# A three-part kernel on one core: the first expert told from one row of its batch, first rows loaded in 1 KB runs, last rows stored in another order, and a new list of steps

## Chip, cores and metric

The kernel runs on one core of a Trainium2 chip. The metric is the device time of one execution in microseconds; shorter is better. Engines are named as in the profile: PE is TensorE (its matmuls; PEld its weight loads), DVE is VectorE, ACT is ScalarE, POOL is GpSimd, SP is SyncE. A name with q (SPq, ACTq) is the engine's instruction queue, which issues transfers.

## What is computed

The reference, cut to what matters (B=4 batches, H=8 heads, S=512 rows, 32 state rows, D=64):

```
a      = softmax(x @ state^T / 8) ; xread = a @ state           # per batch and head
a2     = softmax(state @ x^T / 8) ; sread = a2 @ x
rows   = concat(xread, sread)  -> [4 * 544, 512]
expert = argmax(rows @ w_gate) ; gate = its softmax weight       # 8 experts, 576 places each
mid    = gate * (relu(rows @ w1[expert]) @ w2[expert])           # 512 -> 1024 -> 512; 0 for rows without a place
out    = (silu(mid @ wg) * (mid @ wv)) @ wo                      # 512 -> 1536 -> 512
```

All of it is float32.

## The kernel before

The path `one_expert_a_batch` bets that the 512 x rows of a batch all pick one expert, and its 32 state rows too. It works out these eight experts from counts over all rows, and counts at the end (`verdict`, line 1949) how many of its conditions held. If one did not, the register `bad` is above 0 and a second, general program (`general_path`, line 26) does everything again after it.

The work is cut into small **steps** (`lx`, `xt`, `up` and so on, with a batch number and mostly a piece number). Three lists written out by hand (lines 2311, 2362, 2379) fix the order in which every engine meets them: each engine runs its own instructions in list order and waits on the others only for data or for a free buffer. So a step that waits holds up all that stands behind it on its engine. Weight loads are all issued by SP, in list order as well.

**Attention.** `lx(b)` (line 1549) loads 512 rows of x: row 4p+c goes to partition p, slot c; it is four transfers, one for each c, in runs of 64 values (256 bytes) because x lies head by head. For batch 0 they are split over the SP and the ACT queue, and behind them ACT issues the gate's weights `wgt` and half of the other batches' states. `xt`/`xc` turn x (PE transposes, copies), `sc` makes the scores, `sx`, `mx`, `tt`, `ex2`, `sub`, `ae`, `sn`, `an`, `at`, `ah`, `al` make both softmaxes and split the weights in two float32r parts, `rd` (line 1713) reads x again for the state rows, `lg`, `lc`, `lt` and `ga` to `gf` make the gate's logits, the winner and the places. `ge` (line 1865) writes the expert's number into `e_i`. There are two x buffers (`f_xs`), so the load of batch 2 waits until `rd:0` has read batch 0.

**First expert layer.** `lu(b,z)` (line 1980) reads the expert's number into a register on SP and loads its w1 in four transfers of 512 KB; `ld` loads w2 in four. `z` is 0 for the batch's x rows and 1 for its state rows. `pj` multiplies the states with w1 (the layer is applied to 256 state columns first, since x rows are mixtures of states), `pa`/`pd` split the product, `up`, `hh`, `hl`, `wh`, `wl`, `dn` are the two matmuls in pieces of 128 hidden columns. The state rows take the narrow steps `n1` to `n4l`. A float32 product is three float32r matmuls of high and low parts (`mm3`, line 1464; the matmul itself has line 1466).

**Second layer.** `w2l` loads the 36 pieces of wg, wv, wo; `da`, `db`, `dc`, `dd` rebuild and split each (lines 2217 to 2255); they can begin only when the attention's buffers are given back after `verdict`. `fu`, `fs`, `fm`, `fh`, `fl`, `fd` run batch 0's rows against a piece as soon as it is split. After the lists, `block` (line 2424) runs batch 1, batch 2 and the rest (the last 64 of batch 2's rows, 64 rows of batch 3 and the 128 state rows), and `finish` copies and stores. The state rows stand in the tile `yF` batch after batch, and `rest_rows` stores them so:

```python
o = out.rearrange("(b s) d -> b s d", b=B)[:, S:SEQ]
for b in range(0, B, 2):
    (nc.scalar if b else nc.sync).dma_start(o[b:b + 2], t[NS * b:NS * (b + 2)])
```

Of the kernel before, what the change touches and what calls it, by code (L numbers as in the profile page):

```python
# [1395 lines left out]
def one_expert_a_batch(  # L1396
# [127 lines left out]
    act = ctile([1, 2], "act", pool=const)  # L1524
    nc.scalar.activation(act[:, 0:1], ione[:, 0, 0:1], AF.Exp)
# [22 lines left out]
    @step  # L1548
    def lx(b):

        v[b]["xs"] = xs = xsp.tile([P, NC, DM], F32, tag="xs", name="xs")
        for c in range(NC):
            (nc.scalar if b == 0 and c % 2 else nc.sync).dma_start(
                xs[:, c].rearrange("p (h d) -> p h d", h=H),
                x[b].rearrange("h (p c) d -> c p h d", c=NC)[c],
            )
        if b == 0:
            nc.scalar.dma_start(wgt, w_gate.rearrange("(k p) e -> p k e", p=P))
            for i in range(1, B):
                for g in range(2):  # L1560
                    (nc.scalar if g else nc.sync).dma_start(st_[:, 2 * i + g], state[i, g::2])
# [38 lines left out]
    @step  # L1600
    def xt(b, ks):

        ks = [ks] if b else range(KD)
        for k in ks:
            v[b]["pxt"][k] = bank([P, NC, P], b == 0)
        for c in range(NC):
            for k in ks:
                nc.tensor.transpose(
                    v[b]["pxt"][k][:, c], v[b]["xs"][:, c, k * P:(k + 1) * P], ident
                )  # L1610
# [253 lines left out]
    @step  # L1864
    def ge(b, z):

        n, t = rows_n(z)
        po = v[b]["pq", z]
        nc.vector.tensor_copy(tot[:, b, z], po[0:1, 0])
        w = sm.tile([1, E], F32, tag="t", name="t")  # L1870
        nc.vector.tensor_tensor(w, tot[:, b, z], ione[:, z], op=ALU.mult)
        u = sm.tile([1, 1], F32, tag="u", name="u")
        nc.vector.tensor_reduce(u, w, axis=AX.X, op=ALU.add)
        nc.vector.tensor_copy(e_i[:, 2 * b + z:2 * b + z + 1], u)
        v[b]["places", z] = pl = small(z, "pl", [n, E])
        nc.vector.tensor_copy(pl, po[0:n, 1])
# [433 lines left out]
    with tc.manual_schedule():  # L2310
        run("""
            lx:0 lx:1 st:0 stc:0 xt:0:0 xc:0:0 xc:0:2 st:1 xc:0:1 xc:0:3 xt:1:2 stc:1 sc:0 sg:1
            sx:0:0 mx:0:1 sx:0:1 mx:0:0 ex2:0:1 tt:0:1 ex2:0:0 sgc:1 et:0:1 sub:0:1 xt:1:0
            ec:0:1 rs:0 ae:0:1 et:0:0 xc:1:0 sn:0:1 xc:1:2 tt:0:0 ec:0:0 xt:1:1 an:0:1 sub:0:0
            rd:0 xc:1:1 ae:0:0 at:0:1 lx:2 sr:0 sn:0:0 xt:1:3 ah:0:1 qt:0 sg:0 qc:0 al:0:1
            xc:1:3 an:0:0 sl:0 sgc:0 at:0:0 ga:0:1 sc:1 ah:0:0 gx:0:1 al:0:0 sx:1:0 mx:1:0 lg:0
            sx:1:1 mx:1:1 ex2:1:0 tt:1:1 tt:1:0 sub:1:1 lc:0 et:1:0 ex2:1:1 lt:0 sub:1:0 ae:1:1
            et:1:1 ec:1:0 xt:2:0 ec:1:1 ga:0:0 xt:2:1 gb:0:0 ae:1:0 rd:1 xc:2:0 xc:2:1 gb:0:1
            pq:0:0 gx:0:0 xt:2:3 ge:0:0 pq:0:1 xc:2:3 xt:2:2 sn:1:1 lu:0:0 xc:2:2 ge:0:1 an:1:1
            sn:1:0 at:1:1 ah:1:1 rs:1 an:1:0 ld:0:0:0 gf:0:1 sr:1 ld:0:0:1 ld:0:0:2 qt:1 al:1:1  # L2320
            gd:0:1 at:1:0 qc:1 gf:0:0 pj:0:0 ah:1:0 gd:0:0 al:1:0 pj:0:1 pa:0:0:0 pa:0:0:1
            pd:0:0:0 wh:0:0 pd:0:0:1 wh:0:1 wl:0:0 wl:0:1 lg:1 pa:0:1:1 pa:0:1:0 pd:0:1:1
            pd:0:1:0 sl:1 lc:1 lt:1 ga:1:1 up:0:0 ga:1:0 gx:1:1 gb:1:0 gx:1:0 up:0:1 hh:0:0
# [223 lines left out]
```

## Time and profile before

| | us |
|---|---|
| three runs: median (lowest to highest) | 564.66 (564.31 to 565.61) |
| the profiled execution | 566.21 |
| its span, first to last instruction | 564.6 |
| PE busy in the span | 528.6 (94%) |
| DVE busy | 263.3 (47%) |
| ACT busy | 193.2 (34%) |

The span is what the rows are measured in; 1.6 us of the profiled execution lie around it. All times in rows count from the start of the span. Busy shares are averages over stages with different limits; the stretches tell them apart. PEclk is the granted clock of PE as a share of 2.4 GHz; 0.50 is 1.2 GHz.

### The profile page before, as it was taken

What the parts mean: (1) busy time and instruction counts of PE and PEld (TensorE: products, weight loads), DVE (VectorE), ACT (ScalarE), POOL (GpSimd) and SP (SyncE); (2) the same over time, 40 slices, a digit from 0 to 9 for tenths busy, and PEclk for the clock granted to TensorE, in tenths of its full rate; (3) what the DMA queues carried; (4) which work ended last, traced back from release to release, by engine and by line L of the source; (5) the groups of instructions that cost most, each with busy time, mean ns of one, the idle gap of its engine ahead of it and who ended that gap; (6) DMA issues with size and microseconds to landing.
All of it is one profiled execution on the core that took longest, in us unless ns stands there. A gap on an engine that the chain in (4) does not pass through costs nothing.

```text
span 564.6 us, 8671 instructions
## 1 busy us (share of the span) xinstructions
PE 528.6 (94%) x3402; PEld 430.4 (76%) x3402; DVE 263.3 (47%) x601; ACT 193.2 (34%) x372; POOL 31.7 (6%) x52
## 2 busy tenths in 40 slices
PE   4877999999999997999999999999999999999990
PEld 2654777777787875778888888888888888899990
DVE  2586564657565895799997211111121112231120
ACT  1563444454454653565553211111121111121110
POOL 1110010221030021000000000000000000000000
PEclk9997999999999999999999999999999999999996
DMA  8146694688563978887755500000220000010001
GB/s 162 24 111 210 208 324 134 151 269 287 173 241 128 361 256 259 268 291 212 244 182 165 207 0 1 0 1 0 71 79 2 0 1 0 1 66 1 1 1 43
DMA packets 66968, 72.51 MB, mean 128 GB/s; under 512 B 20389, under 2 KB 51877, under 8 KB 66661
## 3 DMA queue, kind: packets, MB, share of 16 engines
q1 hardware_dynamic: 63634, 70.92, 39.8%
q10 hardware_dynamic: 3282, 0.93, 0.8%
q8 instruction: 29, 0.48, 0.4%
q14 instruction: 23, 0.18, 0.1%
HBM read 62.14 MB, written 9.70 MB: 127 GB/s over the span
## 4 chain that ended last, share of the span: by engine, by line
PE 80%; DVE 7%; DMA 5%; ACT 2%; issue 1%; SPq 1%; POOL 1%; ACTq 1%; POOLq 0%; DVEq 0%
PE m L1466 57%; PE py L1466 13%; DMA rawb<-in_moe_w_dram 2%; DVE hv L2227 1%; DMA yd<-y 1%; DMA f_wgt<-in_moe_w_gate_dram 1%; PE m L2151 1%; PE m L2115 1%; PE py L2453 1%; PE m L1624 1%; DMA rawa<-in_moe_w_dram 1%; DVE hv L2230 1%; DMA xs<-in_x_dram 1%; DVE w L2255 1%; DVE t L2071 1%
## 5 line engine op out<-in xcount | busy, mean ns | idle before, releaser
L2441 DVE TENSOR_TENSOR sg<-sg,m 128x512 f32<-128x512 f32 (+2 forms) x36 | 20.8, 577 | 161.3 <-PE m L1466 161.3
L1466 PE MATMUL m<-xbh,w 128*128 128x512 f32 (+1 forms) x288 | 89.0, 379 | 0.0
L1466 PE MATMUL m<-xc,w 128*128 128x512 f32 (+1 forms) x432 | 77.4, 336 | 0.0
L1466 PEld LDWEIGHTS m<-xc,w 128*128 128x128 f32 x432 | 67.5, 190 | 9.1
L1466 PEld LDWEIGHTS m<-xbh,w 128*128 128x128 f32 x288 | 54.1, 188 | 8.9 <-DVE w L2255 0.4
L1466 PE MATMUL m<-xbl,w 128*128 128x512 f32 (+1 forms) x144 | 54.4, 378 | 0.0
L2440 ACT ACTIVATE sg<-m 128x512 f32<-128x512 f32 (+2 forms) x36 | 18.3, 508 | 104.4 <-PE m L1466 104.4
L1474 ACT CAST hh<-sg 128x512 fp32r<-128x512 f32 (+2 forms) x36 | 19.1, 531 | 85.7 <-DVE sg L2441 85.7
L1466 PE MATMUL py<-w,hh 128*128 128x512 f32 x144 | 44.7, 391 | 0.0
L1466 PE MATMUL m<-hh,wh 128*128 128x512 f32 x96 | 39.5, 412 | 0.0
L1466 PE MATMUL m<-hl,wh 128*128 128x512 f32 x96 | 37.5, 391 | 0.0
L1466 PE MATMUL m<-hh,wl 128*128 128x512 f32 x96 | 37.5, 391 | 0.0
L1466 PE MATMUL m<-ah,wp 128*128 128x512 f32 x96 | 35.5, 419 | 0.0
L1475 DVE TENSOR_TENSOR hl<-sg,hh 128x512 fp32r<-128x512 f32 (+2 forms) x36 | 20.9, 581 | 21.5 <-ACT hh L1474 21.5
L1466 PEld LDWEIGHTS py<-w,hh 128*128 128x128 f32 x144 | 26.5, 188 | 4.9
L1466 PEld LDWEIGHTS m<-xbl,w 128*128 128x128 f32 x144 | 27.1, 188 | 3.9
L1466 PE MATMUL py<-w,hl 128*128 128x512 f32 x72 | 28.1, 390 | 0.0
L2056 DVE TENSOR_TENSOR wl<-rawb,wh 128x512 fp32r<-128x512 f32 x24 | 16.5, 692 | 24.4 <-ACT wh L2051 24.3
L2230 DVE SCALAR_TENSOR_TENSOR hv<-hv 128x512 int32<-128x512 int32 x36 | 25.8, 717 | 3.7
L2227 DVE SCALAR_TENSOR_TENSOR hv<-raw,hv 128x512 int32<-128x512 int32 x36 | 25.9, 719 | 1.2
L2220 ACT ACTIVATE hv<-raw 128x512 f32<-128x512 f32 x36 | 24.1, 677 | 6.4 <-DVE w L2255 4.4
L2250 ACT CAST w<-hv 128x512 fp32r<-128x512 f32 x26 | 16.1, 622 | 27.8 <-DVE hv L2230 22.0
(213 smaller groups left out, 872.6 us busy)
## 6 DMA issues: line engine op xcount, KB each, us to landing
rawa<-in_moe_w_dram SPq DMA_DIRECT2D x32, 512.0 KB, 4.6
rawb<-in_moe_w_dram SPq DMA_DIRECT2D x32, 512.0 KB, 7.0
raw<-in_moe_w_gate_dram SPq DMA_DIRECT2D x12, 512.0 KB, 5.2
raw<-in_moe_w_val_dram SPq DMA_DIRECT2D x12, 512.0 KB, 4.3
raw<-in_moe_w_out_dram SPq DMA_DIRECT2D x12, 512.0 KB, 4.8
yd<-y SPq DMA_DIRECT2D x8, 512.0 KB, 4.9
xs<-in_x_dram SPq DMA_DIRECT2D x14, 256.0 KB, 4.4
out_dram<-ot SPq DMA_DIRECT2D x11, 256.0 KB, 2.1
```

The lines of the kernel that those rows point to most:

```text
L1466: nc.tensor.matmul(po, lh[a], rh[b], start=first and n == 0, stop=last_ and n == 2, tile_position=at)
L1474: nc.scalar.copy(hi, src)
L1475: nc.vector.tensor_tensor(lo, src, hi.bitcast(F32), op=ALU.subtract)
L1624: nc.tensor.matmul(v[b]["pst"][g][NS * k:NS * (k + 1)], sT[D * g:D * (g + 1), b, NS * k:NS * (k + 1)], v[b]["xt"][D * g:D * (g + 1), k], s ...
L2056: nc.vector.tensor_tensor(w[1], raws[b, 0][2][fc // 2][:, fc % 2], w[0].bitcast(F32), op=ALU.subtract)
L2071: nc.vector.tensor_tensor(t, v[b]["py"][j], v[b]["gB"], op=ALU.mult)
L2220: nc.scalar.activation(t[:, 0], Wn[fc, m][0][:, :, 1].bitcast(F32), AF.Copy, scale=2.0 ** -112)
L2227: nc.vector.scalar_tensor_tensor(vi, r[:, :, 0], 29, vi, op0=ALU.logical_shift_right, op1=ALU.bitwise_or)
L2230: nc.vector.scalar_tensor_tensor(vi, hw.bitcast(I32), 3, vi, op0=ALU.logical_shift_left, op1=ALU.bitwise_or)
L2250: nc.scalar.copy(t[:, 0], Wn[fc, m][1][:, 1])
L2440: nc.scalar.activation(sg, ph[0][:, 0:n], AF.Silu)
L2441: nc.vector.tensor_tensor(sg, sg, ph[1][:, 0:n], op=ALU.mult)
```

## The change

1. **The first expert from one row.** Row 0 of batch 0 is loaded by itself (2 KB) and taken through attention and gate ahead of all other rows, in twelve small steps (`q1` to `qe`). The winner goes to `e_i[0]` at once. When `ge:0:0` later has the winner from all rows, it only compares, and the result of the comparison is one more condition in `verdict`.
2. **1 KB runs.** For batches 0 and 1, x is loaded two heads at a time with four rows of a head in one run of 1 KB, into the buffers of later w2 loads (`rawxp`); eight copies (`xg`, half on DVE, half on ACT) put the rows in the order of before.
3. **Queues.** ACT issues only the second half of batch 0's states, row 0 and `wgt`; the states of batches 1 to 3 go on SP behind batch 1's x.
4. **Last rows.** The state rows stand in `yF` in the order (row, batch), written with a stride of 4 columns, and the two last stores each take 16 rows of all four batches.
5. **A new list.** The order of nearly all steps is new. `lu:0:0` stands behind `lx:2` and `rd:0`; `n1:0:1` stands between `up:0:1` and `dn:0:0`; `n3:2:1` and `n4:2:1` stand further apart.

The diff, cut to its core:

```diff
     for g in range(2):
         (nc.scalar if g else nc.sync).dma_start(st_[:, g], state[0, g::2])
+    nc.scalar.dma_start(xrow.rearrange("o (h d) -> o h d", h=H), x[0, :, 0:1].rearrange("h o d -> o h d"))
+    nc.scalar.dma_start(wgt, w_gate.rearrange("(k p) e -> p k e", p=P))
...
-        for c in range(NC):
-            (nc.scalar if b == 0 and c % 2 else nc.sync).dma_start(
-                xs[:, c].rearrange("p (h d) -> p h d", h=H),
-                x[b].rearrange("h (p c) d -> c p h d", c=NC)[c],
-            )
+        if b < 2:
+            v[b]["xw"] = [rawxp.tile([P, 2, 512], F32, tag="raw", name="xw") for _ in range(2)]
+            for k in range(KD):
+                nc.sync.dma_start(
+                    v[b]["xw"][k // 2][:, k % 2].rearrange("p (h m) -> p h m", h=2),
+                    x[b, 2 * k:2 * k + 2].rearrange("h (p c) d -> p h (c d)", c=NC),
+                )
...
+    def xg(b, k):
+        f = nc.scalar.copy if k % 2 else nc.vector.tensor_copy
+        f(
+            v[b]["xs"][:, :, k * P:(k + 1) * P].rearrange("p c (g d) -> p c g d", g=2),
+            v[b]["xw"][k // 2][:, k % 2].rearrange("p (g c d) -> p c g d", g=2, c=NC),
+        )
...
+    def q1():
+        v[0]["q"] = q = bank([P, 512], True)
+        for k in range(KD):
+            nc.tensor.matmul(
+                q[:, k:k + 1], xrow[:, k * P:(k + 1) * P], ones[0:1, 0:1], start=True, stop=True
+            )
...
+    def qg():
+        v[0]["qg"] = qs = [bank([P, E], True) for _ in range(2)]
+        for k in range(KD):
+            for g in range(2):
+                nc.tensor.matmul(
+                    qs[g][NS * k:NS * (k + 1)], sT[D * g:D * (g + 1), 0, NS * k:NS * (k + 1)],
+                    wgt[D * g:D * (g + 1), k], start=True, stop=True,
+                    tile_position=(D * g, NS * k),
+                )
...
+    def qe():
...
+        nc.vector.tensor_scalar(guess[:, 1:2], guess[:, 0:1], float(E), None, op0=ALU.add)
+        nc.vector.tensor_copy(e_i[:, 0:1], guess[:, 1:2])
...
-        nc.vector.tensor_copy(e_i[:, 2 * b + z:2 * b + z + 1], u)
+        if b == z == 0:
+            nc.vector.tensor_tensor(guess[:, 2:3], u, guess[:, 1:2], op=ALU.is_equal)
+        else:
+            nc.vector.tensor_copy(e_i[:, 2 * b + z:2 * b + z + 1], u)
...
+        nc.vector.tensor_tensor(u[:, 0:1], u[:, 0:1], guess[:, 2:3], op=ALU.add)
...
-        return n, col, t, [a[:, :, 64 + col:64 + col + n] for a in yF]
+        at_ = slice(64 + TAIL + b, None, B) if z else slice(64, 64 + TAIL)
+        return n, col, t, [a[:, :, at_] for a in yF]
...
-            lx:0 lx:1 st:0 stc:0 xt:0:0 xc:0:0 xc:0:2 st:1 xc:0:1 xc:0:3 xt:1:2 stc:1 sc:0 sg:1
...
+            lx:0 lx:1 st:0 stc:0 q1 q2 xg:0:0 q3 qg xg:0:1 q4 xt:0:0 qh q5 xg:0:2 xt:0:1 xc:0:0
+            q6 xt:0:2 xg:0:3 xc:0:1 q7 xc:0:2 xt:0:3 xg:1:0 q8 xc:0:3 q9 xg:1:1 qe sc:0 xg:1:2
+            xt:1:1 sx:0:0 mx:0:1 xt:1:0 xg:1:3 mx:0:0 st:1 sx:0:1 ex2:0:1 tt:0:1 stc:1 xt:1:2
+            sub:0:1 xc:1:0 et:0:1 xc:1:1 sg:1 ec:0:1 ae:0:1 tt:0:0 sgc:1 ex2:0:0 sn:0:1 xt:1:3
+            xc:1:2 et:0:0 xc:1:3 sub:0:0 sg:0 an:0:1 ec:0:0 at:0:1 sgc:0 ae:0:0 rs:0 rd:0 ah:0:1
+            sn:0:0 sc:1 lx:2 sr:0 al:0:1 an:0:0 qt:0 sx:1:1 mx:1:1 qc:0 at:0:0 sx:1:0 mx:1:0
+            sl:0 ah:0:0 lu:0:0 tt:1:0 ga:0:1 ex2:1:1 al:0:0 tt:1:1 ex2:1:0 sub:1:0 lg:0 gx:0:1
...
+            gx:1:1 xt:2:1 pa:0:0:0 at:1:1 pa:0:0:1 pd:0:0:0 gd:0:1 pq:0:0 ah:1:1 gp:0:1 ld:0:0:0
+            pd:0:0:1 xc:2:1 ld:0:0:1 al:1:1 pj:0:1 gc:0:1 ge:0:0 lg:1 pa:0:1:0 gf:0:0 pa:0:1:1
+            up:0:0 lc:1 pd:0:1:0 gd:0:0 pd:0:1:1 lt:1 hh:0:0 hl:0:0 up:0:1 ga:1:0 gb:1:0 gx:1:0
+            n1:0:1 hh:0:1 gb:1:1 wh:0:0 hl:0:1 wh:0:1 pq:1:0 pq:1:1 n1a:0:1 ge:1:0 gp:0:0 n2:0:1
+            wl:0:0 gc:0:0 lu:1:0 sc:2 n2a:0:1 ge:1:1 dn:0:0 sx:2:1 wl:0:1 sx:2:0 gf:1:0 mx:2:1
...
-            o = out.rearrange("(b s) d -> b s d", b=B)[:, S:SEQ]
-            for b in range(0, B, 2):
-                (nc.scalar if b else nc.sync).dma_start(o[b:b + 2], t[NS * b:NS * (b + 2)])
+            o = out.rearrange("(b s) d -> s b d", b=B)[S:SEQ]
+            for i in range(2):
+                (nc.scalar if i else nc.sync).dma_start(
+                    o[NS // 2 * i:NS // 2 * (i + 1)], t[64 * i:64 * (i + 1)]
+                )
```

## Rows read from the trace of the kernel before

**Rows 1.** Stretches of the span: length, busy time by engine, granted clock, DMA.
```profile
core 0: us, PE busy (x) PEld busy (x) DVE busy (x) ACT busy (x) POOL busy (x), PEclk, DMA share, GB/s
0.00:60.00 60.00, 41.89 (x453) 29.40 (x453) 32.61 (x112) 25.99 (x56) 7.91 (x30) 0.91 0.48 119
60.00:260.00 200.00, 195.22 (x1448) 148.85 (x1448) 137.40 (x323) 97.88 (x190) 23.76 (x22) 1.00 0.75 242
260.00:551.50 291.50, 291.50 (x1505) 252.11 (x1503) 92.90 (x168) 68.93 (x125) 0.00 (x0) 1.00 0.17 56
...
180.00:300.00 120.00, 116.44 (x679) 92.48 (x679) 103.43 (x183) 64.96 (x112) 5.53 (x4) 1.00 0.82 262
```

**Rows 2.** Chain of waits that ended last, first 64 us: start, length, what.
```profile
3.45 6.18 DMA f_wgt<-in_moe_w_gate_dram
...
16.07 2.02 PE m L1624 x16
...
21.45 0.85 PE m L1608 x4
...
41.15 8.54 DMA rawb<-in_moe_w_dram
...
59.35 0.35 PE m L1862 x4
...
61.09 2.73 PE m L1466 x12
```

**Rows 3.** Instructions in order of time, first 62 us: start, length, engine, line.
```profile
24.79 1.10 PE L1713 MATMUL m<-xs,e2t 128*32 128x64 f32 x64
...
25.95 2.86 SPq L1553 DMA_DIRECT2D xs<-in_x_dram  x4
...
26.32 0.60 PE L1608 MATMUL m<-f_ident,xs 128*128 128x128 f32 x4
...
38.87 2.10 SPq L1987 DMA_DIRECT2D rawa<-in_moe_w_dram  x4
...
44.69 0.68 DVE L1757 TENSOR_TENSOR al<-m,ah 128x512 fp32r<-128x512 f32 x1
...
52.37 1.78 PEld L1797 LDWEIGHTS m<-f_add,lgr 128*128 128x128 f32 x8 [2.81 <-ACT lgr L1790]
```

**Rows 4.** Stretches of the first 60 us, columns as in rows 1.
```profile
5.00:6.00 1.00, 0.87 (x4) 0.72 (x4) 0.00 (x0) 0.00 (x0) 0.00 (x0) 1.00 1.36 223
...
44.00:46.00 2.00, 1.48 (x32) 0.40 (x16) 1.27 (x7) 0.67 (x2) 1.04 (x1) 0.68 1.09 362
...
52.40:59.00 6.60, 6.60 (x20) 5.54 (x21) 3.25 (x16) 1.03 (x3) 0.00 (x0) 0.50 0.00 0
```

**Rows 5.** Groups of instructions: line, engine, form, count | busy us, mean ns | idle before.
```profile
L1617 DVE COPY xt<-m 128x512 f32<-128x512 f32 x2 | 1.3, 685 | 5.2 <-PE m L1608 5.2
...
L1640 DVE TENSOR_SCALAR mx<-mx 128x1 f32<-128x1 f32 x8 | 1.2, 154 | 0.3
```

**Rows 6.** Instructions in order of time, end of the span.
```profile
551.49 0.56 ACTq L2481 DMA_DIRECT2D out_dram<-ot  x1
...
552.96 0.63 SPq L2485 DMA_DIRECT2D out_dram<-ot  x1
```

**Rows 7.** One stretch while the last stores run, columns as in rows 1.
```profile
557.00:558.00 1.00, 0.00 (x0) 0.00 (x0) 0.00 (x0) 0.00 (x0) 0.00 (x0) 0.50 0.16 47
```

**Rows 8.** Line 2481's transfer to landing; SP's waits behind the path (line 2514).
```profile
DMA to landing us min/median/max: 2.9/2.9/2.9
...
L2514 SPq EVENT_SEMAPHORE  x9: 17/17/17, 556.5 to 562.9; - x9
```

**Rows 9.** Who waited for whom: PE from 60 to 310 us; SP, whole span.
```profile
PE m L2167 <- ACT ny L2161: 3.0, 1, 3.0
...
SPq L2210 <- DVE f_bad_i L1959: 9.7, 1, 9.7
```

**Rows 10.** The page's chain of work, by line, whole span.
```profile
PE m L1466 57%; PE py L1466 13%; DMA rawb<-in_moe_w_dram 2%; DVE hv L2227 1%; DMA yd<-y 1%; DMA f_wgt<-in_moe_w_gate_dram 1%; PE m L2151 1%; PE m L2115 1%; PE py L2453 1%; PE m L1624 1%; DMA rawa<-in_moe_w_dram 1%; DVE hv L2230 1%; DMA xs<-in_x_dram 1%; DVE w L2255 1%; DVE t L2071 1%
```

More of the change, by code (lines that the diff above doesn't have):

```diff
@@ L1559, in lx @@
+        if b == 1:
             for i in range(1, B):
                 for g in range(2):
-                    (nc.scalar if g else nc.sync).dma_start(st_[:, 2 * i + g], state[i, g::2])
+                    nc.sync.dma_start(st_[:, 2 * i + g], state[i, g::2])
+    @step
+    def xg(b, k):
[4 more added lines that the diff above has]
+        )
@@ new lines, in q1, with q2, q3 @@
+    @step
+    def q1():
[4 more added lines that the diff above has]
+            )
+    @step
+    def q2():
+        for g in range(2):
+            r = slice(D * g, D * (g + 1))
+            nc.vector.tensor_copy(xq[r, g], v[0]["q"][r, 0:KD])
+    @step
+    def q3():
+        v[0]["qs"] = q = bank([P, 2, KD, NS], True)
+        for g in range(2):
+            for k in range(KD):
+                nc.tensor.matmul(
+                    q[0:1, g, k], xq[:, g, k:k + 1], sT[:, 0, NS * k:NS * (k + 1)],
+                    start=True, stop=True,
+                )
@@ new lines, in row8, with q4, q5 @@
+    def row8(a):
+        return a.unsqueeze(2).to_broadcast([1, H, NS])
+    @step
+    def q4():
+        s = v[0]["qs"][0:1].rearrange("o g k n -> o (g k) n")
+        v[0]["qd"] = d = wk.tile([1, H, NS], F32, tag="lgr", name="qd")
+        v[0]["qm"] = m = sm.tile([1, H], F32, tag="qm", name="qm", bufs=1)
+        nc.vector.tensor_reduce(m, s, axis=AX.X, op=ALU.max)
+        nc.vector.tensor_tensor(d, s, row8(m), op=ALU.subtract)
+    @step
+    def q5():
+        nc.scalar.activation(v[0]["qd"], v[0]["qd"], AF.Exp, scale=scale)
@@ new lines, in q6, with q7 @@
+    @step
+    def q6():
+        d, m = v[0]["qd"], v[0]["qm"]
+        nc.vector.tensor_reduce(m, d, axis=AX.X, op=ALU.add)
+        nc.vector.tensor_scalar(m, m, 1e-9, None, op0=ALU.add)
+        nc.vector.reciprocal(m, m)
+        nc.vector.tensor_tensor(d, d, row8(m), op=ALU.mult)
+    @step
+    def q7():
+        v[0]["qt"] = q = bank([P, 512], True)
+        d = v[0]["qd"].rearrange("o h n -> o (h n)")
+        for g in range(2):
+            nc.tensor.matmul(
+                q[:, g:g + 1], d[:, P * g:P * (g + 1)], ones[0:1, 0:1], start=True, stop=True
+            )
@@ new lines, in q8 @@
+    @step
+    def q8():
+        nc.vector.tensor_copy(aq, v[0]["qt"][:, 0:2])
+    @step
+    def qg():
+        v[0]["qg"] = qs = [bank([P, E], True) for _ in range(2)]
+        for k in range(KD):
+            for g in range(2):
+                nc.tensor.matmul(
+                    qs[g][NS * k:NS * (k + 1)], sT[D * g:D * (g + 1), 0, NS * k:NS * (k + 1)],
+                    wgt[D * g:D * (g + 1), k], start=True, stop=True,
+                    tile_position=(D * g, NS * k),
+                )
@@ new lines, in qh, with q9 @@
+    @step
+    def qh():
+        for g in range(2):
+            nc.vector.tensor_copy(gq[:, g], v[0]["qg"][g])
+    @step
+    def q9():
+        v[0]["ql"] = q = bank([P, E], True)
+        for g in range(2):
+            nc.tensor.matmul(q[0:1], aq[:, g:g + 1], gq[:, g], start=g == 0, stop=g == 1)
+    @step
+    def qe():
+        l = v[0]["ql"][0:1]
+        o = sm.tile([1, E], F32, tag="qo", name="qo", bufs=1)
+        nc.vector.tensor_reduce(guess[:, 0:1], l, axis=AX.X, op=ALU.max)
+        nc.vector.tensor_tensor(o, l, guess[:, 0:1].to_broadcast([1, E]), op=ALU.subtract)
+        nc.vector.scalar_tensor_tensor(
+            o, o, 0.0, w8[0:1], op0=ALU.is_equal, op1=ALU.mult
+        )
+        nc.vector.tensor_reduce(guess[:, 0:1], o, axis=AX.X, op=ALU.max)
+        nc.vector.tensor_scalar(guess[:, 0:1], guess[:, 0:1], 1.0, -1.0, op0=ALU.max, op1=ALU.mult)
+        nc.vector.tensor_scalar(guess[:, 1:2], guess[:, 0:1], float(E), None, op0=ALU.add)
+        nc.vector.tensor_copy(e_i[:, 0:1], guess[:, 1:2])
@@ L1600, in xt @@
     @step
[L1601 to L1605, printed above, removed]
+    def xt(b, k):
+        v[b]["pxt"][k] = bank([P, NC, P], b == 0)
         for c in range(NC):
[L1607 to L1610, printed above, removed]
+            nc.tensor.transpose(
+                v[b]["pxt"][k][:, c], v[b]["xs"][:, c, k * P:(k + 1) * P], ident
+            )
     @step
@@ L2318, in one_expert_a_batch @@
[L2318 to L2323, printed above, removed]
```

148 lines of the change are left out of this document (77 added, 71 removed).

## The prediction

> **What bounds the kernel now.** I read the busy times by stretch first. PE is busy in all of 260 to 551.5 us and in 195.2 of the 200 us before; only the first 60 us (18.1 us idle) and the 13.1 us behind its last matmul leave much to gain [rows 1]. So a microsecond saved ahead of 260 us counts only if PE's whole stream moves up by it, and a store at the end counts in full.
>
> Next the chain of waits for the first 60 us. It runs through the load of `wgt` (3.45 to 9.63 us), to the scores `sc:0` at 16.07, through batch 0's attention, and then sits in one transfer: a w2 piece of the first expert, 41.15 to 49.69 [rows 2]. The loads of that expert's w1 are issued at 38.87, since its number comes from counts over all 512 rows [rows 3]. Batch 1's attention is through at 45.37 (`al`, [rows 3]), but copies for the late weights stand ahead of `lc:1` on ACT, and `lt:1` on PE waits 2.8 us for it until 52.4 [rows 3]. What follows, `up:0:0` and `up:0:1`, runs at the lower level: from 52.4 to 59.0 the granted clock is 0.50, that is 1.2 GHz, after PE stood idle for those 2.8 us [rows 3, 4]. At 59.70 (end of the four matmuls of line 1862) both `up` are done [rows 2]; this is the mark by which I compare.
>
> **The front, step by step.** *To `sc:0`.* Runs of 256 bytes saturate the transfers: 223 GB/s at a DMA share of 1.36; runs of 1 KB, as the expert's w1 has them, moved 362 GB/s [rows 4]. Batch 0's 1 MB would take 2.9 us in place of 4.7, batch 1's the same, and batch 1's transposes no longer stand ahead of `sc:0` waiting for their rows. But the new list puts `qg`, which needs `wgt`, ahead of the first transpose. Today `wgt` lands at 9.63, behind two 256 KB loads on ACT's queue [rows 2]; without them I take 7.5. Its bounds are 5.5 (2 us after it is issued) and 9.6, as now; the value lies in the middle, because it still shares the engines with x. From 7.5: `qg` 0.5, three times four transposes at 0.85 [rows 2], `q7`, four more, one DVE copy of 0.69 [rows 5]: **sc:0 at 12.5** in place of 16.07. The other costs of the guess lie in this stretch. Four `xg` on DVE are priced at the 685 ns of the nearest copy [rows 5] (bounds 0.3 and 0.7, source and target both in SBUF), two of them ahead of `sc:0`. The small DVE steps are some 18 instructions of 0.15 [rows 5], 2.7 us, most of them while DVE would wait for transposes (it idles 5.2 us there now, [rows 5]). PE gets 24 one-column matmuls, below 1 us. What hides them is the wait for x and `wgt`; without it they would add some 2 us to the way to `sc:0`.
>
> *`sc:0` to the end of `rd:0`.* Now 16.07 to 25.89. The new list has more PE work in between: the scores 2.0, nine times four transposes at 0.85, `st:1` 1.3, both `sg` 1.3, `rd` 1.1, together 13.4 us. That holds at the slow pace of the start; four transposes take 0.85 us there [rows 2] and at 26.3 no more than 0.60, their last one's tail included [rows 3]. If the pace changes after as much dense work as now, about 10 us, the end lies near 23; with none, at 25.9. DVE has some 10 us of its own work there. I take **24.5**.
>
> *First weights.* `lx:2` follows on SP, four issues in 2.9 us as now [rows 3], then the register, then four loads: issued by 30, and landed by some 36, behind 1 MB in short runs. The new list wants them at `pj:0:0` near 38. So the guess, there from about 13, isn't what sets the load; `rd:0` is, through the x buffer, and all the same the load comes 9 us earlier.
>
> *To `up:0:0`.* From `rd:0`'s end to batch 1's last `al` takes 45.37 - 25.89 = 19.5 us now, with DVE and PE both four fifths busy; nothing of it goes. That gives 44.0, `lg:1` 45.0. Then `up` twice 2.73 for both [rows 2], `lt:1` 1.0 at full pace, the four counts 0.35: **49.1 against 59.70, a gain of 10.6 us.** The `pj`, `pa`, `pd` of both halves fall into gaps of the same 19.5 us; if they don't, up to 3 us go. Bounds: `wgt` early and an early pace give 14; `wgt` as now and 1.2 GHz again around 45 give 7. Moved loads count too: six state loads now pass SP behind batch 1's x, at 0.63 each [rows 6] some 4 us of SP, due for `st:1` at about 16; `lu:0:1`'s four w1 loads now go ahead of the first w2 pieces, which should land near 47 and are due for `dn:0:0` at about 53. Behind SP's wait for `rd:0` stand only these expert loads.
>
> **The middle.** From 60 to 260 us PE idles 4.8 us [rows 1], 3.0 of it in one wait of `n4:2:1` for a copy on ACT [rows 9]; the new list puts other work between those two steps. It can also make new gaps: every step is moved, and DVE is busy 103.4 of the 120 us from 180 to 300, PE 116.4 [rows 1]. I take no change, with bounds of -3.5 (nearly all idle goes) and +5 (as much again). The stride-4 writes into `yF` and the one more condition are five short ACT and DVE instructions and one of 0.15, off PE's path.
>
> **The tail.** The last two stores are issued at 552.96 [rows 6], 128 KB each. While they run, the DMA share is 0.16, so 2.6 of 16 engines, at 47 GB/s; SP's last wait ends at 562.9 [rows 7, 8], and 1.7 us follow. The store of the same size from 64 partitions one step earlier, on ACT's queue and beside another on SP, landed in 2.9 us [rows 6, 8]. Both differ from the last ones in the shape of the target: they walk 64 rows, the last ones two blocks. The new stores walk 16 rows of four batches. If they land like line 2481's, data is there at 555.9, before SP's first wait at 556.5 [rows 8]; with 0.6 for SP's other waits and the 1.7, the span ends at 558.8 in place of 564.6: **a gain of 5.8.** Bounds: 0 (spread as now) and 6.4 (only landing counts). I take the upper part, because the row of the same size and queue is the nearest. The Trainium skill, "DMA: Bandwidth & Descriptors", "Why a DMA increments its semaphore by 16 and not by 1", says that a transfer runs on the largest number of engines, up to 16, that divides the slowest dimension on both sides: 2 for the old stores, 16 for the new. By the rows alone the gain could be anything from 0 to 6.4; by that rule it is the whole.
>
> **The sum.** 10.6 + 0 + 5.8 = 16.4. Against the profiled execution of 566.21 (span 564.6) that is 549.8; the median of the runs lies 1.55 below that execution, so I forecast 564.66 - 16.4 = **548.3 us**.
>
> **Rivals.** *The second layer takes the front's gain back* (0.12). The conversion of its weights begins when `verdict` gives the buffers back; SP waits 9.7 us for it now [rows 9]. If batch 3's attention doesn't come earlier with the rest, DVE's 103 us of work from there on end as late as now, PE waits for split pieces, and the front counts for nothing: 564.66 - 5.8 = 558.9. For it: DVE's load there. Against it: `verdict` stands behind about as many `up` and `dn` in the new list, and all of these move.
>
> *The last stores spread as before* (0.10), and so the change doesn't do this part: 564.66 - 10.6 = 554.1. Against it stands line 2481's row.
>
> *Slower: the guess misses* (0.03). Row 0's logits come from other products in another order than the batch's. Where its two best experts lie closer than this rounding, the comparison in `ge:0:0` fails, `bad` is 1, and the general program runs behind the path. Its price is at least the matmuls again, 70% of 564.6 or 395 us [rows 10]: above 940 us. From the first wrong comparison on it decides all. Against it: all 512 rows of the batch agree in the runs of before, or the general path would show in the span.
>
> **How the numbers follow.** My case has 0.75, with its own range of 542 to 554 by the bounds above taken together two at a time. The missing tail lies at 554.1 and the lost front at 558.9; up to 557 I leave out most of the latter, the guess and the far ends, below 0.2 in all. So the range is 542 to 557. A measurement of this kernel tells about 0.2% from no change, 1.1 us. Faster by more: 0.75 + 0.12 + 0.10 less a little for surprises, 0.95; within it 0.02; slower 0.03.
>
> **What would show it.** Right: `sc:0` near 12.5, first w1 loads issued near 28, `up:0:0` near 45 with no stretch at 0.50 behind it, two `up` and four counts done by 49; PE idle of about 5 us between there and 250; SP's last wait within 4 us of the last issue. Wrong: PE waiting for `wgt` beyond 9.6; w2 pieces that land after 53; PE idle growing from 170 to 250 behind DVE; or a DMA share of 0.16 over many microseconds at the end.

## The result and the profile after

The changed kernel takes **545.34 us** (median of four runs, 544.21 to 547.22) against 565.13 beside it: a ratio of 0.9647, interval 0.9612 to 0.9681. The forecast was 548.3 in a range of 542 to 557. Timed twice more, beside the experiments, it took 547.13 and 546.67 us (ratios 0.966 and 0.9659).

The profiled execution took 547.22 us with a span of 545.6, so 19.0 us less span than before. By stretches (columns as in [rows 1]):

```profile
core 0: us, PE busy (x) PEld busy (x) DVE busy (x) ACT busy (x) POOL busy (x), PEclk, DMA share, GB/s
0.00:60.00 60.00, 49.89 (x584) 36.36 (x585) 43.95 (x166) 33.98 (x74) 9.72 (x33) 0.97 0.60 188
60.00:260.00 200.00, 197.50 (x1482) 152.75 (x1481) 145.85 (x319) 100.56 (x194) 22.43 (x20) 1.00 0.70 235
260.00:535.00 275.00, 275.00 (x1379) 238.93 (x1378) 76.37 (x138) 57.81 (x107) 0.00 (x0) 1.00 0.15 49
535.00:545.60 10.60, 2.17 (x10) 1.44 (x8) 0.85 (x2) 1.33 (x3) 0.00 (x0) 0.81 0.20 57
```

PE's idle time fell from 18.1 to 10.1 us in the first 60 us and from 4.8 to 2.5 us in the next 200; its busy time fell from 528.6 to 524.6, although steps were added, which fits the granted clock of the first 60 us (0.97, before 0.91; at 0.50 PE runs at 1.2 GHz). Those are 14.4 us. The other 4.6 lie behind PE's last matmul, which now ends at 537.17, 8.4 us ahead of the end (before 13.1).

**The front.** The chain of waits (start, length, what) begins elsewhere than forecast:

```profile
2.09 3.48 DMA f_xrow<-in_x_dram
...
5.62 1.88 PE m L1593 x8
...
7.80 1.01 PE m L1608 x16
8.81 0.25 PE m L1655 x16
9.06 2.75 PE m L1729 x12
11.81 0.84 PE m L1641 x4
12.65 0.58 PE m L1729 x4
13.23 0.18 PE m L1670 x4
13.41 1.71 PE m L1745 x16
```

Line 1593 is `q1`, 1608 `q3`, 1655 `qg`, 1641 `q7`, 1745 `sc:0`. `qg`, the step that needs `wgt`, follows `q3` with no wait: `wgt` holds nothing up. What does is row 0's landing at 5.57 and the guess's own matmuls with one row or column, 1.88 + 1.01 + 0.84 = 3.7 us of PE. The marks in order of time (start, length, engine, line):

```profile
22.58 1.92 PE L1834 MATMUL m<-xs,e2t 128*32 128x64 f32 x64
...
24.59 2.82 SPq L1571 DMA_DIRECT2D xs<-in_x_dram  x4
28.18 2.09 SPq L2113 DMA_DIRECT2D rawa<-in_moe_w_dram  x4
...
43.76 0.40 PE L1466 MATMUL m<-ah,wp 128*128 128x512 f32 x1
...
47.53 2.00 PE L2241 MATMUL m<-rawa,f_sTs 128*32 128x256 f32 x32
49.46 0.62 PE L1983 MATMUL m<-f_cc,f_ones 128*128 128x16 f32 x4
```

`rd:0` ends at 24.50, the first expert's w1 loads are issued at 28.18 (before 38.87, [rows 3]), `up:0:0` starts at 43.76 at full speed. The mark of the prediction (both `up` and the four counts, 59.70 before) falls at 50.08; but the new list put `n1:0:1` ahead of the counts, 1.93 us of PE. Without it the mark is 48.15, a gain of 11.5 us.

One piece of the front still runs at 1.2 GHz (columns as above):

```profile
22.00:23.00 1.00, 1.00 (x22) 0.83 (x26) 0.90 (x9) 0.94 (x2) 0.00 (x0) 0.83 0.00 0
23.00:24.00 1.00, 1.00 (x49) 1.00 (x44) 0.93 (x4) 0.27 (x1) 0.00 (x0) 0.50 0.08 25
24.00:26.00 2.00, 2.00 (x36) 0.48 (x28) 0.57 (x2) 0.52 (x2) 1.05 (x1) 0.50 0.07 17
```

It comes behind two waits of PE, 0.62 us before 20.28 and 0.70 before 22.00. `rd:0` takes 1.92 us in it, 1.10 at full clock [rows 3].

**The middle.** Who waited for whom, PE, 60 to 260 us:

```profile
PE m L2256 <- ACT ny L2250: 1.6, 1, 1.6
...
PE m L2293 <- ACT ny L2287: 0.2, 1, 0.2
```

Line 2293 is `n4`, which waited 3.0 us before [rows 9]: 0.2 are left. What is left of the stretch's idle time is mostly a wait of `n2:3:0` (line 2256) for ACT.

**The tail.** The last two stores, in order of time:

```profile
538.62 0.57 SPq L2614 DMA_DIRECT2D out_dram<-ot  x1
538.63 0.63 ACTq L2614 DMA_DIRECT2D out_dram<-ot  x1
```

Stretches behind them, columns as above:

```profile
538.60:539.50 0.90, 0.00 (x0) 0.00 (x0) 0.00 (x0) 0.00 (x0) 0.00 (x0) 1.00 0.76 219
539.50:540.50 1.00, 0.00 (x0) 0.00 (x0) 0.00 (x0) 0.00 (x0) 0.00 (x0) 1.00 0.57 182
540.50:541.50 1.00, 0.00 (x0) 0.00 (x0) 0.00 (x0) 0.00 (x0) 0.00 (x0) 0.99 0.36 113
541.50:542.50 1.00, 0.00 (x0) 0.00 (x0) 0.00 (x0) 0.00 (x0) 0.00 (x0) 0.50 0.05 12
```

Who waited for whom, SP, from 535 us on:

```profile
SPq L2645 <- SPq L2645: 4.1, 2, 2.9
```

The DMA view from 541.5 to the end, busy share in 40 slices, then the queues with their packets:

```profile
DMA  0000201010030020000000000000000000000000
...
q14 instruction: 3, 0.02, 1.9%
q10 hardware_dynamic: 5, 0.01, 1.1%
```

The first of these stretches still holds the two stores before them, which were issued at 537.14. The last two moved 182 GB/s at a share of 0.57 in the second stretch, where the old ones moved 47 at 0.16 [rows 7], and are all but done at 541.5, 2.9 us behind their issue. The packet times in the trace say the same: in the kernel before never more than three packets of 2 KB are under way at once from 554.2 to 561.7, here up to 18 from 539.8 to 541.2. Behind 541.5 come four more rows of ACT's store (queue q10, until 542.9) and three instruction packets, the last from 543.0 on; 2.5 us later the span ends. From the last issue to the end are 7.0 us, before 11.6.

Of the nine profiles compared below, this and one other have such late rows. SP's waits behind the path (line 2645), here and in the second and third profile of the changed kernel (both below), from the first to the last:

```profile
L2645 SPq EVENT_SEMAPHORE  x9: 17/17/17, 542.2 to 543.9; - x9
...
L2645 SPq EVENT_SEMAPHORE  x9: 17/17/17, 544.8 to 545.4; - x9
...
L2645 SPq EVENT_SEMAPHORE  x9: 17/17/17, 541.3 to 541.9; - x9
```

In these other two the last rows have landed 2.6 and 2.4 us behind the last issue, 1.4 and 1.2 us ahead of SP's first wait, and from the last issue to the end are 6.2 and 5.9 us.

### The profile page after: what moved, and what is told of

Read it like the earlier page. It is cut to its first block, busy times and chain, and to the rows that moved or that the text cites. A ratio compares the mean times of both kernels' runs of the same rounds, so it can differ in the third digit from the quotient of the medians.

```text
span 545.6 us, 8802 instructions
## 1 busy us (share of the span) xinstructions
PE 524.6 (96%) x3450; PEld 429.5 (79%) x3450; DVE 267.0 (49%) x624; ACT 193.7 (36%) x377; POOL 32.1 (6%) x53
## 4 chain that ended last, share of the span: by engine, by line
PE 85%; DVE 5%; DMA 5%; ACT 2%; POOL 1%; issue 1%; ACTq 0%; SPq 0%; DVEq 0%; POOLq 0%
PE m L1466 60%; PE py L1466 13%; DMA raw<-in_moe_w_gate_dram 3%; PE m L2277 2%; PE m L2241 1%; PE m L2139 1%; PE py L2582 1%; DMA yd<-y 1%; PE m L1745 1%; PE m L2042 1%; PE m L1834 1%; DMA f_xrow<-in_x_dram 1%; PE m L1859 1%; PE m L1729 1%; PE m L1903 0%
## 5 line engine op out<-in xcount | busy, mean ns | idle before, releaser
L2177 ACT CAST wh<-rawb 128x512 fp32r<-128x512 f32 x24 | 14.7, 620 | 30.2 <-PE m L1466 27.1
L1466 PE MATMUL m<-xbh,w2r 128*128 128x512 f32 (+1 forms) x80 | 24.6, 377 | 0.0
```

What stands on the lines that cost most here:

```text
L1466: nc.tensor.matmul(po, lh[a], rh[b], start=first and n == 0, stop=last_ and n == 2, tile_position=at)
L2177: nc.scalar.copy(w[0], raws[b, 0][2][fc // 2][:, fc % 2])
```

## The experiments

Of twelve kernels eight are the changed kernel with an edit, two the kernel before with one part of the change, two the changed kernel as it is. The kernel before was timed beside each group (565.55, 566.96 and 566.19 us).

**The changed kernel again** (no edit), as the measure for the next four.

> The changed kernel once more, beside the three others, as their level. All theories: 545.3 us (544 to 547), ratio to before 0.965.

547.13 us (545.11 to 548.76), ratio 0.966 [0.9614, 0.9707]. Its profiled span is 547.1, with `up:0:0` at 44.56 in place of 43.76: `sc:0` took 2.52 us here (1.73 in the first profile) and `rd:1` 1.93 (1.10), the latter with a granted clock of 0.72 from 32 to 36 us. So the pace of the front's pieces differs from one execution to the next, and with it one or two microseconds.

**The old last rows in the changed kernel.**

```diff
-        at_ = slice(64 + TAIL + b, None, B) if z else slice(64, 64 + TAIL)
-        return n, col, t, [a[:, :, at_] for a in yF]
+        return n, col, t, [a[:, :, 64 + col:64 + col + n] for a in yF]
...
-            o = out.rearrange("(b s) d -> s b d", b=B)[S:SEQ]
-            for i in range(2):
-                (nc.scalar if i else nc.sync).dma_start(
-                    o[NS // 2 * i:NS // 2 * (i + 1)], t[64 * i:64 * (i + 1)]
-                )
+            o = out.rearrange("(b s) d -> b s d", b=B)[:, S:SEQ]
+            for b in range(0, B, 2):
+                (nc.scalar if b else nc.sync).dma_start(o[b:b + 2], t[NS * b:NS * (b + 2)])
```

> The changed kernel with the last 128 rows in the order of before, stored as two batches of 32 rows in each of two stores. Theory (the shape of the target made the last stores slow, and that is all of the tail's gain): 4.6 us more than the changed kernel, near 549.9; from the last store's issue to the end of the span 11.6 us as in the kernel before, DMA share near 0.16 there, 7.0 now. Rival (the tail is shorter for another reason, as where the code behind the path lies): within 1 us of the changed kernel.

550.09 us (549.25 to 551.98), ratio 0.9736 [0.9693, 0.9779]: 3.0 us above the changed kernel by the medians, 4.3 by the ratios. A stretch behind the last stores, columns as above:

```profile
540.00:541.00 1.00, 0.00 (x0) 0.00 (x0) 0.00 (x0) 0.00 (x0) 0.00 (x0) 0.50 0.16 47
```

Who waited for whom, SP, from 534 us on:

```profile
SPq L2642 <- SPq L2642: 8.5, 2, 5.7
```

The share of 0.16 and the long wait are back, and the last issue (536.03) lies 11.5 us ahead of the end, as before.

**The new last rows alone**, in the kernel before: the reverse of that edit.

> The kernel before with the changed order of the last rows and their two stores alone. Theory (the old stores run on 2 of the 16 engines and hold back the end): last issue to end falls from 11.6 to some 7 us, the time by 4 to 5 us, ratio 0.991 to 0.993. Rival (the end is held by something behind the stores): under 2 us, ratio above 0.9965.

561.79 us (560.44 to 564.68), ratio 0.9929 [0.9901, 0.9956]: 4.4 us. Last issue at 552.12, span 558.9, so 6.8 us in place of 11.6. In the stretch of [rows 7], a microsecond behind the issue:

```profile
553.00:554.00 1.00, 0.00 (x0) 0.00 (x0) 0.00 (x0) 0.00 (x0) 0.00 (x0) 0.72 0.54 172
```

The tail is worth 4.4 us by itself, and 3.0 to 4.3 when it is taken away; from the last issue to the end it saves 4.5 to 5.7 in the profiles. The changed kernel without it gains 15.5 us by medians (565.55 - 550.09); 15.5 and 4.4 are 19.9, and the whole change gained 18.4 to 19.8 us by medians in its three timings. Within 1.5 us the parts add up.

**The guess alone, with the old list** (and the old runs, copies and stores): the twelve steps stand in the old list, and `lu:0:0` behind `lx:2`.

```diff
-            lx:0 lx:1 st:0 stc:0 xt:0:0 xc:0:0 xc:0:2 st:1 xc:0:1 xc:0:3 xt:1:2 stc:1 sc:0 sg:1
+            lx:0 lx:1 st:0 stc:0 q1 q2 q3 q4 q5 q6 xt:0:0 xc:0:0 xc:0:2 st:1 xc:0:1 xc:0:3 qg qh q7 q8 q9 qe xt:1:2 stc:1 sc:0 sg:1
...
-            rd:0 xc:1:1 ae:0:0 at:0:1 lx:2 sr:0 sn:0:0 xt:1:3 ah:0:1 qt:0 sg:0 qc:0 al:0:1
+            rd:0 xc:1:1 ae:0:0 at:0:1 lx:2 lu:0:0 sr:0 sn:0:0 xt:1:3 ah:0:1 qt:0 sg:0 qc:0 al:0:1
...
```

> The kernel before with the guess alone: row 0's steps behind its load, lu:0:0 right behind lx:2; old list otherwise, old loads of x, old tail. Theory: first w1 load issued near 29, landed by 36, lc:1 no longer behind late weights, up:0:0 near 48 in place of 54.1 and at 2.4 GHz: 6.5 to 9.5 us less than before, 556 to 558.5. Rival (the new list is needed to make use of early weights): 3 us less than before or nothing.

559.27 us (557.92 to 559.51), ratio 0.9879 [0.9837, 0.9921]: 6.3 us by medians, 6.8 by the ratio, at the lower edge of the theory's interval and well above the rival's. In order of time:

```profile
28.71 3.13 SPq L2096 DMA_DIRECT2D rawa<-in_moe_w_dram  x4
...
49.09 1.06 PE L1902 MATMUL m<-f_add,lgr 128*128 128x8 f32 x8 [0.72 <-ACT lgr L1895]
50.01 0.48 PE L1466 MATMUL m<-ah,wp 128*128 128x512 f32 x1
```

The loads are issued as early as in the changed kernel (28.71), but `up:0:0` starts only at 50.01: with the weights there, the old list's attention sets it. `lt:1` waits 0.72 us in place of 2.81, and the matmuls behind it run at full clock.

**The loads told from the counts, with the rest of the change.** `qe` writes no expert, `ge:0:0` does, and `pq:0:0 ge:0:0 lu:0:0` stand ahead of `rd:1`.

```diff
-        nc.vector.tensor_copy(e_i[:, 0:1], guess[:, 1:2])
...
         if b == z == 0:
             nc.vector.tensor_tensor(guess[:, 2:3], u, guess[:, 1:2], op=ALU.is_equal)
-        else:
-            nc.vector.tensor_copy(e_i[:, 2 * b + z:2 * b + z + 1], u)
+        nc.vector.tensor_copy(e_i[:, 2 * b + z:2 * b + z + 1], u)
...
-            gb:0:0 rd:1 gx:0:0 at:1:0 gb:0:1 ah:1:0 xt:2:0 rs:1 pq:0:1 al:1:0 sr:1 xt:2:2 ge:0:1
+            gb:0:0 pq:0:0 ge:0:0 lu:0:0 rd:1 gx:0:0 at:1:0 gb:0:1 ah:1:0 xt:2:0 rs:1 pq:0:1 al:1:0 sr:1 xt:2:2 ge:0:1
...
```

> The changed kernel, but the first expert's loads wait for the counts over all rows again, which the list now has right behind gb:0:0; row 0 is still worked out and compared. Theory (the early load matters, but the new list hides part of a late one): first w1 load issued near 36.5 in place of 28.2, landed by 43, up:0:0 at 45.5 to 48 in place of 43.8, 2 to 6 us more than the changed kernel, the upper half if PE's clock falls to 1.2 GHz in the wait. Rival A (the front's gain is the earlier scores and the list, the guess is worth nothing): within 0.7 us of the changed kernel. Rival B (the guess carries the whole front): 9 us or more.

553.76 us (551.86 to 555.73), ratio 0.978 [0.9728, 0.9832]: 6.6 us above the changed kernel, somewhat more than the theory had. In order of time:

```profile
34.96 0.58 PE L1982 MATMUL m<-f_cc,f_ones 128*128 128x16 f32 x2 [3.15 <-DVE f_cc L1974]
...
37.08 8.06 SPq L2111 DMA_DIRECT2D rawa<-in_moe_w_dram  x7
...
50.81 0.63 PE L1466 MATMUL m<-ah,wp 128*128 128x512 f32 x1
```

The stretches behind that first wait and around `up:0:0`, columns as above:

```profile
36.00:40.00 4.00, 4.00 (x68) 3.83 (x58) 2.21 (x15) 1.48 (x4) 0.00 (x0) 0.50 0.43 134
...
50.00:52.00 2.00, 2.00 (x6) 1.61 (x5) 1.01 (x2) 0.76 (x2) 0.00 (x0) 0.50 1.07 366
```

The loads go out at 37.08, PE waits 0.30 and 0.55 us for their pieces and 2.25 ahead of `pj:0:1`, which the profile puts down to a DVE step (line 2016), and `up:0:0` comes at 50.81 and at 1.2 GHz. Not all of this is due to late weights: the counts stand ahead of `rd:1` here, PE waits 3.15 us for them and runs at 1.2 GHz behind that, so that `rd:1` ends at 37.41, 1.7 to 4.3 us later than in the three profiles of the changed kernel. So the guess is worth 6.3 us in the old list, and 6.6 in the new against this one place of the counts, clock included; other places were not tried. The new order and the queues are worth the other 7 to 9 (this kernel gains 11.8, less 3.0 to 4.4 for the tail); they were not tried apart.

**Short runs, no copies**, the rest as changed: `if b < 2` in `lx` becomes `if False`, and `xg` returns at once.

> The changed kernel with x of batches 0 and 1 loaded in 256-byte runs again, on SP, straight into place, and without the eight copies. Theory (the long runs are worth little by themselves: the first transpose waits behind row 0's steps on PE until 9 us, when short runs have landed too, and only batch 1's rows come later): 0.5 to 2.5 us more than the changed kernel. Rival A (they carry the front): 4 us more or above. Rival B (the copies cost as much as the runs save): within 0.5 us, or less time.

547.42 us (545.41 to 551.88), ratio 0.9669 [0.9634, 0.9704], against 0.9647 to 0.966 with the long runs: no difference that can be told, though the interval leaves room for some 2 us either way. The time alone would also fit the rival by which the copies cost what the runs save. `sc:0` starts at 13.38 (with them 13.34), and ahead of it the chain of waits of both kernels has row 0, the guess's matmuls and the transposes, and no load of the batch: the 1 KB runs are off the path there.

**Idle transposes to fill PE**, at the start (`q1` and `st:0`), behind the scores (`et`, `at`), and both. They write where the step's own transposes write afterwards.

```diff
+    def spin(to, n):
+        for _ in range(n):
+            nc.tensor.transpose(to, zero, ident)
...
+        spin(q[:, P:2 * P], 4)
...
+        if i == 0:
+            spin(pt[:, 1], 12)
...
+        if (b, g) == (0, 0):
+            spin(pe2[:, 0], 6)
...
+        if (b, g) == (0, 1):
+            spin(pat[:, 0], 6)
```

> The changed kernel with 12 transposes of a zero tile ahead of the first state transpose and 4 ahead of q1, into parts of their banks that are written anew or never read. Theory (PE's work from 5.6 to 12 us, 7 us of it, runs at the lower level because PE had done nothing before, and it is on the path): the pace changes by some 8 us in place of 12.6, sc:0 ends 1.5 to 2.5 us earlier, the time falls by 1 to 2.5 us. Rival (that stretch is set by the copies and softmax steps on DVE and ACT): within 0.5 us.

> The changed kernel with 6 zero transposes ahead of et:0:0 and 6 ahead of at:0:1, where PE waits 0.6 and 0.7 us. Theory (the half level from 22.6 to 26 us follows these waits, and doubles rd:0 and sc:1 on the path): granted clock 1.00 from 20 to 30 us, the time falls by 1.5 to 3 us, and its runs lie closer together than the 4 us of now. Rival (the level falls for another reason or the stretch is covered): within 0.5 us.

> Both sets of zero transposes. Theory: the gains add, 2.5 to 5 us less than the changed kernel, 540 to 544. Rival (with an earlier start other steps set the pace, so that the second set finds no wait): no better than the better one of the two alone.

At the start: 544.29 us (543.71 to 548.6), ratio 0.962 [0.9587, 0.9653]. In the middle: 545.76, 0.9612 [0.9582, 0.9641]. Both: 548.48, 0.9681 [0.9651, 0.9711]. The first two lie 2 to 3 us lower by their ratios than the changed kernel, which was timed with another group (0.9659 [0.9628, 0.9689]); the intervals overlap, so a gain isn't shown. The third has a granted clock of 1.00 in all of the first 60 us and `up:0:0` at 41.83, and yet isn't faster. The transposes aren't needed for that clock: the kernel with the old last rows and the first one of the next group have the changed kernel's list there and none of them, and read the same, with `up:0:0` at 41.52 and 41.79. The latter's row, columns as above:

```profile
0.00:60.00 60.00, 49.66 (x602) 36.11 (x610) 45.13 (x169) 34.63 (x76) 9.70 (x33) 1.00 0.64 200
```

A part of what the third won (0.9 to 1.4 us more than in the changed kernel's profiles) is lost at one wait, in order of time:

```profile
217.18 0.66 PE L2267 MATMUL m<-f_ident,ny 128*128 128x128 f32 x4 [2.46 <-ACT ny L2261]
```

It is `n2:3:0` again. What ACT was late for stands in the chain of waits of the changed kernel:

```profile
206.62 8.76 DMA raw<-in_moe_w_gate_dram
...
215.46 0.67 ACT hv L2348
216.13 0.49 ACT ny L2250
...
216.66 0.66 PE m L2256 x4
```

The relu that `n2:3:0` needs stands on ACT behind `da:4:0`, which waits for a piece of the second layer that takes 8.8 us to come.

**That wait taken away**: `n2:3:0` behind two steps that are ready, in the changed kernel and in the one with transposes at the start; the changed kernel once more beside them.

```diff
-            db:3:2 fu:3:0 da:4:0 n1a:3:0 db:4:0 w2l:5:0 dc:3:2 ld:3:0:2 n2:3:0 fs:3 fu:3:1
+            db:3:2 fu:3:0 da:4:0 n1a:3:0 db:4:0 w2l:5:0 dc:3:2 ld:3:0:2 fs:3 fu:3:1 n2:3:0
```

> The changed kernel once more, as the measure for the other three on the same chip. Both theories: 545 to 547 us, ratio 0.963 to 0.967, and one wait of 1.5 to 2.5 us of n2:3:0 on PE between 200 and 220 us (line 2256, for ACT's relu).

> The changed kernel with one step moved: n2:3:0 behind fs:3 and fu:3:1. Theory A (the wait is one of order alone: ACT's relu n1a:3:0 stands behind da:4:0, which waits for a weight piece, and PE waits at n2:3:0 with fu:3:1 ready behind it): the wait of 1.6 us goes, PE is busy in all of 200 to 260, the time falls by 1.2 to 2.0 us against the changed kernel beside it (ratio near 0.962). Theory B (the second layer's pieces come at the pace of their transfers and DVE, and PE has no lead): a wait of 1 to 2.5 us for a piece (w, line 2383, or hv) stands at the next fu or fd between 215 and 260, and the time stays within 0.7 us.

> The same move on top of the kernel with idle transposes at the start. Theory A (the front's gain was lost only at n2:3:0): 1.5 to 3.5 us below the changed kernel beside it, 542 to 544 us, ratio 0.957 to 0.961; it would be the fastest of all. Theory B (pieces at their own pace): within 1 us of the changed kernel, the wait moved to a piece of the second layer.

546.67, 545.86 and 545.62 us; ratios 0.9659 [0.9628, 0.9689], 0.9647 [0.9616, 0.9677] and 0.9638 [0.9606, 0.967]. The step no longer waits, but eight microseconds later another one does, here in the first of the two kernels:

```profile
224.05 0.50 PE L1466 MATMUL m<-w,hl 128*128 128x512 f32 x1 [1.52 <-DVE hl L2412]
```

The wait is as long as the one taken away (1.57 in the first profile, 1.10 beside). The times are 0.8 and 1.1 us below the kernel beside them, short of theory A's 1.2 and 1.5, and the intervals are too wide to choose by the time alone. By the trace theory B is right that the wait moves, but not in what it is for: it isn't a piece but `hl`, a product of the rows' own path, which stands on DVE behind its work on two pieces. DVE is busy 37.8 of the 40 us from 220 to 260 there. None of these versions is shown to beat the changed kernel.

Across the nine profiled executions with the new list and the early load, the front's gain still mostly reached the end. The start of `up:0:0`, PE's longest wait from 200 to 260 us, the start of DVE's last copy, and this less the first:

| | up:0:0 | wait | last copy | difference |
|---|---|---|---|---|
| changed, first | 43.76 | 1.57 | 538.17 | 494.41 |
| changed, second | 44.56 | 1.1 | 540.43 | 495.87 |
| changed, third | 42.44 | 1.10 | 537.23 | 494.79 |
| short runs | 42.26 | 1.39 | 537.00 | 494.74 |
| transposes at the start | 41.86 | 0.90 | 536.04 | 494.18 |
| transposes in the middle | 44.35 | none | 538.41 | 494.06 |
| transposes in both places | 41.83 | 2.46 | 538.67 | 496.84 |
| `n2:3:0` later | 41.79 | 1.52 | 536.52 | 494.73 |
| the same, transposes at the start | 43.09 | 1.52 | 537.42 | 494.33 |

In seven of the nine the difference lies within 0.8 us, and the front's gain came through whole, also where `up:0:0` starts some 2 us ahead of the first profile. In the one with transposes in both places 2.1 to 2.8 us went in between, and its wait is the longest; but in the changed kernel's second profile 1.1 to 1.8 went with a wait of 1.1, so this wait isn't all of it.

## Why the prediction was right

By its own steps, against 16.4 us forecast and 19.0 measured in the span:

- **The front, 10.6 forecast, 11.5 measured.** The size and the order were right: `rd:0` ends at 24.50 as forecast, the first w1 loads go out at 28.18 (near 28), `up:0:0` starts at 43.76 (45), and no stretch at 0.50 follows it. `rd:0`, not the guess, sets the loads, as said. From `rd:0`'s end to `up:0:0` are 19.3 us (20.5 forecast). The two runs on the guess put the early load at 6.3 to 6.6 us of the time, with the clock behind the waits; the rest, by difference, belongs to the new order and the queues.
- **To `sc:0`: 12.5 forecast, 13.34 measured, and by another cause.** The step that failed is "`wgt` at 7.5": it was not waited for. The term that was mis-sized is the guess's own PE work, "24 one-column matmuls, below 1 us": `q1`, `q3` and `q7` alone (28 records in the trace) took 3.7 us. Four `xg` on DVE took 411 ns on average, not 685, inside the bounds of 0.3 and 0.7.

```profile
L1583 DVE COPY xs<-xw 128x512 f32<-128x512 f32 x4 | 1.6, 411 | 0.0
```

- **The pace** changed earlier than I took: four transposes last 0.65 us at 12.58, where I had 0.85 for all ahead of `sc:0`. The stretch at 1.2 GHz from 23 to 26 gave some of it back. These errors nearly cancel in `rd:0`'s end; that it looks exact is luck.
- **The 1 KB runs** were the first term of the way to `sc:0`. Short runs give the same `sc:0` and no time that can be told, so that term is worth nothing on this way: row 0's load and the guess's matmuls fill the time.
- **The middle, 0 forecast, 2.9 measured** (14.4 to PE's end less 11.5), inside the bound of 3.5; 2.3 of it is PE's idle time from 60 to 260 us, the rest has no row. I had named its main part, the wait of `n4:2:1` (3.0 to 0.2 us), and then counted it at nothing, against the gaps that a new list can make. The sign "PE idle of about 5 us" up to 250 missed with it (2.5 are left). A new wait of 1.6 us came at `n2:3:0`, so the fear of new gaps wasn't idle either.
- **The tail, 5.8 forecast, 4.6 measured in the first profile** (by the experiments' times 3.0 to 4.4). The mechanism was right, and in the second and third profile its terms come out nearly as priced: the rows land 2.4 to 2.6 us behind the issue (2.9 forecast, as line 2481's store), SP's waits last 0.6 us and 1.7 follow, and from the last issue to the end are 6.2 and 5.9 us, where the forecast makes it 5.8. In the first profile the term that was off is the landing of the last four rows, 4.3 us behind the issue; SP's waits last 1.7 us there and the end comes 7.0 behind the issue. SP's last wait lies 4.2 to 5.3 us behind the last issue, so the sign "within 4 us" missed narrowly. That stores of this order keep more transfers going at once is what the shares show, 0.16 before and 0.57 now, and the packets, three at most and up to 18. The Trainium skill, "DMA: Bandwidth & Descriptors", "Why a DMA increments its semaphore by 16 and not by 1", has a transfer use the largest number of engines that divides both sides' slowest dimension; the trace agrees in direction (0.16 against 0.57), and no row here counts the engines. Where the rows land ahead of SP's first wait, what sets the end is not shown; that it waits for the code behind the path is a guess for which only the instruction packets among the last ones speak.
- **The rivals.** The last stores did not spread as before. The guess held. The second layer didn't take the front's gain back, and two kernels with `up:0:0` some 2 us earlier still (transposes at the start, `n2:3:0` later) kept that too. A third, with transposes in both places, lost 2.1 to 2.8 us on the way, a part of it in a wait for ACT, which there is busy with the second layer's pieces. What sets the length of these waits, none to 2.5 us, stays open.

## What to carry to other kernels

Before the last store, compare the rows of its stretch with those of another store of the same size: a DMA share of 0.16 named a loss of some 3 to 4 us that an order of rows gave back. When a load is brought forward, look for the next item that its user needs: here the early weights alone were worth 6.3 us, until the attention set the start, and the new order and queues another 7 to 9, with early weights or without. A wait of an in-order list that is taken away by moving one step may come back one step later, so judge such a move by the stretch's idle time and not by the wait.

## What was not expected of the hardware

The same kernel ran other pieces of its first 60 us at the lower level in each of three profiles: the granted clock is 0.83 and 0.74 from 20 to 24 and 24 to 28 us in the first, 0.72 and 0.85 from 32 to 36 and 36 to 40 in the second, 0.60 from 32 to 36 in the third. With idle transposes they lie elsewhere again (0.72 from 6 to 12 us with those at the start, 0.79 and 0.78 between 32 and 40 with those in the middle), and two kernels without them (old last rows, `n2:3:0` later) read 1.00 in all of the first 60 us. So one profile of a stretch at the lower level doesn't say what an edit there would give back.

The pace of the first 15 us isn't in these figures. The granted clock reads 1.00 there, and yet four transposes took 1.12 us at 13.18 in the second profile, 0.65 at 12.58 in the first. `sc:0` took 1.73 us in six of the nine executions above and 2.52 to 2.60 in three; the same 16 matmuls for batch 1 (`sc:1`) took 1.09 at 1.00 later. A part of the 1.73 is a wait: the last four weight loads of `sc:0` start at 14.02, behind a copy on DVE that ends at 13.96. Matmuls with one row are slow there too: the eight of `q1` took 1.88 us, more than `sc:0` with 512 columns each (1.73).
